# A table of powers moved into an accumulation bank, and the state product put into the bank of the query-key products

## The chip, the core and the metric

The kernel runs on one core of one Trainium2 chip. The metric is the device time of one execution in microseconds (us), the median of several executions. A core has five engines here: PE (TensorE, matrix products), DVE (VectorE), ACT (ScalarE), POOL (GpSimd) and SP (SyncE, which issues the DMAs). Each works through its own list of instructions in order. PE writes into eight accumulation banks (PSUM), all else that the engines read and write lies in SBUF.

## The reference

Three layers, one after the other, in float32, for a batch of 4, 768 positions, 8 heads of 48:

```python
for t in range(S):                                  # attention with a decaying state, per head
    kt, vt, rt = k[:, :, t], v[:, :, t], r[:, :, t]
    cur = einsum('bhd,bhe->bhde', u * kt, vt)
    y[:, :, t] = einsum('bhd,bhde->bhe', rt, state + cur)
    state = w[:, :, None] * state + einsum('bhd,bhe->bhde', kt, vt)
x = y as (4, 768, 384)
h = maximum(x @ w_in, 0); u, v = halves of h        # gate over positions, width 1024 -> 512
v_n = (v - mean) / sqrt(var + 1e-6)
x = (u * (w_spatial @ v_n + b_spatial)) @ w_out
h = maximum(x @ w_in2, 0)                           # gate with a convolution of 3 positions
x = (h * sigmoid(conv(h, conv_w))) @ w_out2
```

## The kernel before, in words

The attention is cut into 24 chunks of 128 positions, 6 for each batch entry. Chunk n has its queries and keys transposed in `ld[n]` (112 partitions: two heads of 48 with 16 unused between them; 4 pairs of heads by 128 positions), and queries, keys and values by position in `nat[n]`. The decay inside a chunk is put into tables of powers of `w`: `TT[:, 0]` for the queries, w to the power t - 64, and `TT[:, 1]` for the keys, w to the power 63 - t, which is the first one read backwards. A chunk goes through these steps:

- `scaled` (L569): the queries by their table on VectorE (L574), the keys by theirs on GpSimd (L583). For chunk 0 both at once on VectorE (L578).
- `bonus` and `keys` (L586, L604): GpSimd forms r*k*u (L591, L593) and scales the keys for the state (L606); VectorE sums the former (L249), and ScalarE lays the sums on the diagonal of `aT` (L254).
- `products` (L211): 8 products of keys and queries into two banks, `pa[0]` for the first head of each pair and `pa[1]` for the second. `masked` (L618) then copies each bank's valid triangle into `aT` on VectorE (L621).
- `outer` (L235): the product of keys and values over the chunk into the bank `pu`; `state` (L677) adds it to `zc` on VectorE (L683, L685), and ScalarE copies `zc` into `zbd` (L245) once `from_state` has read the old one; GpSimd decays `zc` (L692).
- `from_state` (L219) and `from_chunk` (L225): the result, summed in the bank `py`, which ScalarE and VectorE then split into two parts (L658 to L662).

The eight banks are all given away: three to the big products, one to the conversion of the weights, four to the attention (`pa[0]`, `pa[1]`, `py`, `pu`).

All other products of the kernel are done three times on such split parts. s1 (L709) and s2 (L755) multiply the attention's result by `w_in`, s3 (L776) goes over the positions, s4 (L800) multiplies by `w_out`, s5 (L878) and s6 (L921) are the second gate. The weights of the first gate come as 64-bit floats and are converted bit by bit on VectorE (L427 to L430) before they are split by ScalarE and GpSimd (L362, L364).

The order on every engine is set when the program is built: `Order` is a planner that goes through the steps with costs (`vector(cols)` is cols/960 + 0.17 us, `pairs(us)` is given by hand), and gives each engine the waiting step of lowest rank. `need` waits for keys that other steps announce by `done`. `od.chain` sets steps of TensorE one behind the other up to their `FORK`: one chain of `att_a` (the products, L609) and one of `att_v` (state product, from_state, from_chunk; L624). Where the planner has nothing for TensorE in its first 62 us, `keep_warm` (L558) puts in products of the identity that nobody reads. Other work comes into the gaps by rank, so the attention of later batch entries runs among the big products.

Of the kernel before, what the change touches and what calls it, by code (L numbers as in the profile page):

```python
# [26 lines left out]
class Order:  # L27
# [13 lines left out]
    @staticmethod  # L41
    def need(*keys):
        return "need", keys
# [42 lines left out]
    def spawn(self, g, rank=1, at=None):  # L86
        self._go(g, rank, self.t if at is None else at, None)
# [61 lines left out]
class Net:  # L149
# [28 lines left out]

    def att_psum(self, ps):
        C, NP = self.C, self.NP  # L180
        self.pa = [ps.tile([C, NP, C], F32, name=f"pa{i}") for i in range(2)]
        self.py = ps.tile([self.R, NP, C], F32, name="py")
        self.pu = ps.tile([self.R, NP, self.D], F32, name="pu")
        self.nc.vector.memset(self.py, 0.0)
        self.nc.vector.memset(self.pu, 0.0)

# [161 lines left out]
    def run(self, xd=None):  # L348
# [130 lines left out]
        if xd is None:  # L479
            ac = right("ac", 1)  # L480
            ld_p, nat_p = right("ld", 3), right("nat", 3)
            ew_p, at_p, ys_p = right("ew", 2), right("at", 2), right("ys", 2)
            TT = ac.tile([R, 2, NP, C], F32, name="TT")
            W128 = ac.tile([R, NP, 1], F32, name="W128")
            mask = ac.tile([C, C], U32, name="mask")
            maskb = mask.rearrange("c (o t) -> c o t", o=1).to_broadcast([C, NP, C])
            yd = dram.tile([n_chunks, R, 2 * C], F32, name="yd")
            W128b = W128.to_broadcast([R, NP, D])
# [19 lines left out]
        def tables():  # L508
# [14 lines left out]
            nc.vector.memset(wk, 1.0)  # L523
            self.att_psum(att.enter_context(tc.tile_pool(name="ps_a", bufs=1, space=PSUM)))

# [12 lines left out]
            nc.vector.reciprocal(out=iv, in_=asc[:, :, HALF:HALF + 1])  # L538
            nc.vector.tensor_tensor(TT[:, 0, :, 0:HALF], asc[:, :, 0:HALF], ivb, ALU.mult)
            nc.vector.tensor_tensor(TT[:, 1, :, HALF:C], dsc[:, :, 1:HALF + 1], ivb, ALU.mult)  # L540
            nc.scalar.activation(out=TT[:, 0, :, HALF:C], in_=asc[:, :, 0:HALF], func=ACTF.Copy)
            nc.scalar.activation(out=TT[:, 1, :, 0:HALF], in_=dsc[:, :, 1:HALF + 1], func=ACTF.Copy)

            for p in range(NP):
                nc.scalar.activation(
                    out=dw[:, p], in_=self.ident[0:R, 0:R], func=ACTF.Copy, scale=W128[:, p])
            self.transpose_table(TT[:, 1], dw)

# [20 lines left out]
        def scaled(n):  # L569
            yield need(("ldd", n))  # L570
            if n:
                spawn(scaled_k(n), rank(n))
                yield dve(NP * C)
                nc.vector.tensor_tensor(ld[n][:, 0], ld[n][:, 0], TT[:, 0], ALU.mult)  # L574
                done(("lq", n))
            else:
                yield dve(2 * NP * C)
                nc.vector.tensor_tensor(ld[n], ld[n], TT, ALU.mult)  # L578
                done(("lq", n), ("lk", n))

        def scaled_k(n):
            yield gps(NP * C)
            nc.gpsimd.tensor_tensor(ld[n][:, 1], ld[n][:, 1], TT[:, 1], ALU.mult)  # L583
            done(("lk", n))
# [24 lines left out]
        def att_a(n):  # L609
            yield need(("lq", n), ("lk", n))  # L610
            yield need(("A", n - 1, 0), ("A", n - 1, 1))
            yield od.pairs(1.0)
            self.products(ld[n][:, 0], ld[n][:, 1])
            for x in range(2):
                spawn(masked(n, x), rank(n))
            yield FORK

# [6 lines left out]
        def att_v(n):  # L624
            b, c = divmod(n, NCH)
            on = c < NCH - 1
            yield need(("lq", n), ("kn", n), ("z", n - 1))
            if on:
                yield od.pairs(0.45)
                self.outer(nat[n][:, 1], nat[n][:, 2])  # L630
                spawn(state(n), rank(n))
            yield need(("y", n - 1))
# [3 lines left out]
            done(("mix", n))  # L636
            yield need(("A", n, 0), ("A", n, 1))
            if c % HC == 0:
# [38 lines left out]
        def state(n):  # L677
            first = n % NCH == 0
            if not first:
                yield need(("zw", n - 1))  # L680
            yield dve(NP * D)
            if first:
                nc.vector.tensor_copy(out=self.zc, in_=self.pu)  # L683
            else:
                nc.vector.tensor_tensor(self.zc, self.zc, self.pu, ALU.add)  # L685
            yield need(("mix", n))
            yield act(2 * NP * D, 2)
            self.set_state()
            done(("z", n))
            if n % NCH < NCH - 2:  # L690
                yield gps(NP * D)
                nc.gpsimd.tensor_tensor(self.zc, self.zc, W128b, ALU.mult)  # L692
                done(("zw", n))
# [265 lines left out]

        done(("A", -1, 0), ("A", -1, 1), ("z", -1), ("y", -1))  # L960
        by_gat = gat_p, "g", gat_f, 2 * HT
# [39 lines left out]
        if xd is None:  # L1001
# [4 lines left out]
            for n in range(3):  # L1006
                spawn(load(n), rank(n))
                spawn(scaled(n), rank(n))
                spawn(bonus(n), rank(n))
            for g in (att_a, att_v):  # L1010
                spawn(od.chain([(g(n), rank(n)) for n in range(n_chunks)]), 0)
        else:
# [110 lines left out]
```

## Time and profile before

| what | value |
|---|---|
| median of 3 executions | 602.54 us (599.0 to 602.73) |
| profiled execution, its own time | 605.17 us |
| its span, first to last instruction | 603.1 us |
| PE busy | 577.6 us (96%) |
| DVE, ACT, POOL busy | 382.3, 356.5, 291.2 us |
| granted TensorE clock, mean over the span | 0.976 |

The profile is of one execution. The span is what lies between its first and its last instruction; the rest of its own time lies around it. Busy time counts an engine's instructions, not the waits between them.

### The profile page before, as it was taken

To read this page: it belongs to the slowest core of one execution; us is meant where nothing else is said; L and a number is where in the kernel's file an instruction comes from. 1 tells how busy PE (TensorE), PEld (TensorE's weight loads), DVE (VectorE), ACT (ScalarE), POOL (GpSimd) and SP (SyncE) were. 2 spreads that over 40 slices of the span, in tenths; PEclk is the share of its full clock that TensorE was granted. 3 is DMA by queue.
4 is the path that set the end of the run, shared out by engine and by line. 5 is a ranking of instruction groups with operands and counts; after the bars stand their busy time and mean duration, and the time that the engine had idled before them with its cause. 6 is when DMAs were issued, how large, how long until landed. Compare 5 with 4: busy or idle time off the path is not lost.

```text
span 603.1 us, 11155 instructions
## 1 busy us (share of the span) xinstructions
PE 577.6 (96%) x3980; PEld 546.3 (91%) x3980; DVE 382.3 (63%) x864; ACT 356.5 (59%) x877; POOL 291.2 (48%) x315
## 2 busy tenths in 40 slices
PE   6999969999999999999999999999999999999992
PEld 3999858999888999888999999999999999999991
DVE  4889878867679847778665533675546455564701
ACT  3558766736586456486354524487667666675810
POOL 5688877855858329468414240254223243232410
PEclk8999969999999999999999999999999999999997
DMA  8676545546565456285346714340221303120010
GB/s 219 209 218 210 153 158 163 172 140 212 156 194 195 114 165 217 57 265 160 120 166 238 261 59 139 150 158 27 93 84 49 106 13 106 57 76 27 15 39 33
DMA packets 49316, 81.29 MB, mean 135 GB/s; under 512 B 5601, under 2 KB 40930, under 8 KB 48866
## 3 DMA queue, kind: packets, MB, share of 16 engines
q1 hardware_dynamic: 49250, 80.48, 42.3%
q8 instruction: 33, 0.54, 0.4%
q14 instruction: 33, 0.27, 0.1%
HBM read 57.27 MB, written 23.20 MB: 133 GB/s over the span
## 4 chain that ended last, share of the span: by engine, by line
PE 88%; POOL 3%; DMA 3%; DVE 2%; issue 1%; ACT 1%; SPq 0%; ACTq 0%; DVEq 0%; POOLq 0%
PE s L887 17%; PE s L933 17%; PE s L784 15%; PE s L720 9%; PE s L810 8%; PE s L764 7%; PE pa L216 4%; PE warm L565 4%; PE py L231 4%; PE py L222 2%; DMA ld<-in_rkT_dram 1%; PE pu L239 1%; DMA nat<-in_rkv_dram 1%; POOL nat L591 1%; POOL ld L583 1%
## 5 line engine op out<-in xcount | busy, mean ns | idle before, releaser
L364 POOL TENSOR_TENSOR g<-g,g 128x384 fp32r<-128x384 f32 x64 | 64.6, 1014 | 122.6 <-ACT g L362 122.6
L887 PE MATMUL s<-xl,wi 128*128 128x386 f32 x576 | 108.1, 340 | 0.0
L933 PE MATMUL s<-wo,g 128*128 128x384 f32 x576 | 107.0, 339 | 0.0
L784 PE MATMUL s<-wsp,vn 128*128 128x384 f32 x576 | 104.3, 337 | 0.4 <-POOL vn L364 0.4
L887 PEld LDWEIGHTS s<-xl,wi 128*128 128x128 f32 x576 | 102.5, 189 | 0.0
L933 PEld LDWEIGHTS s<-wo,g 128*128 128x128 f32 x576 | 102.1, 188 | 0.0
L784 PEld LDWEIGHTS s<-wsp,vn 128*128 128x128 f32 x576 | 99.7, 188 | 2.4 <-POOL vn L364 0.8
L900 DVE SCALAR_TENSOR_TENSOR c<-h,cw,c 128x384 f32<-128x384 f32 x64 | 39.7, 621 | 57.6 <-ACT c L898 57.6
L254 ACT ACTIVATE aT<-ident,dg 128x128 f32<-128x128 f32 x192 | 60.1, 392 | 9.3 <-DVE dg L249 9.0
L364 POOL TENSOR_TENSOR gat<-u,gat 128x384 fp32r<-128x384 f32 x32 | 32.6, 1027 | 53.7 <-ACT gat L362 49.4
L720 PE MATMUL s<-wi,xT 128*128 128x512 f32 x216 | 57.2, 415 | 0.0
L764 PE MATMUL s<-xT,wi 128*128 128x384 f32 x288 | 54.7, 338 | 0.0
L810 PE MATMUL s<-gat,wo 128*128 128x384 f32 x288 | 53.3, 337 | 0.0
L764 PEld LDWEIGHTS s<-xT,wi 128*128 128x128 f32 x288 | 50.0, 188 | 1.0 <-ACT zbd L245 0.2
L810 PEld LDWEIGHTS s<-gat,wo 128*128 128x128 f32 x288 | 50.0, 188 | 0.6 <-ACT zbd L245 0.2
L720 PEld LDWEIGHTS s<-wi,xT 128*128 128x128 f32 x216 | 41.6, 198 | 9.5 <-issue 0.2
L903 ACT ACTIVATE c<-c 128x384 f32<-128x384 f32 x64 | 29.7, 465 | 31.5 <-DVE c L901 31.5
L907 DVE TENSOR_TENSOR g<-h,c 128x384 f32<-128x384 f32 x64 | 35.2, 551 | 19.9 <-ACT c L903 18.8
L895 ACT ACTIVATE h<-s 128x386 f32<-128x386 f32 x64 | 31.3, 489 | 17.1 <-PE s L887 15.9
L901 DVE SCALAR_TENSOR_TENSOR c<-h,cw,c 128x384 f32<-128x384 f32 x64 | 39.9, 623 | 2.3
L591 POOL TENSOR_TENSOR nat<-nat 128x384 f32<-128x384 f32 x24 | 24.9, 1039 | 31.6 <-DMA nat<-in_rkv_dram 23.3
L364 POOL TENSOR_TENSOR stg<-stg 128x192 fp32r<-128x192 f32 (+1 forms) x34 | 19.8, 587 | 41.2 <-ACT stg L362 35.7
(103 smaller groups left out, 932.1 us busy)
## 6 DMA issues: line engine op xcount, KB each, us to landing
nat<-in_rkv_dram SPq DMA_DIRECT2D x24, 576.0 KB, 4.2
ld<-in_rkT_dram SPq DMA_DIRECT2D x24, 448.0 KB, 5.4
xl<-x2d SPq DMA_DIRECT2D x8, 1155.0 KB, 6.1
x2d<-x SPq DMA_DIRECT2D x24, 384.0 KB, 3.0
stg<-in_w_out_dram SPq DMA_DIRECT2D x24, 192.0 KB, 2.8
out_dram<-o SPq DMA_DIRECT2D x24, 192.0 KB, 1.9
stg<-in_w_in_dram SPq DMA_DIRECT2D x12, 256.0 KB, 3.9
wo2d<-stg SPq DMA_DIRECT2D x16, 192.0 KB, 1.9
```

The costliest lines, as they stand in the source:

```text
L254: self.nc.scalar.activation(out=a[:, x, h // 2], in_=self.ident, func=ACTF.Copy, scale=d[:, h:h + 1])
L364: nc.gpsimd.tensor_tensor(dst[1], src, dst[0].bitcast(F32), ALU.subtract)
L720: nc.tensor.matmul(out=ps, lhsT=xt[:, k, l], rhs=wi[:, k, r, UF:DFF], start=(k == 0 and (l, r) == PARTS[0]), stop=(k == KD - 1 and (l, r) ...
L764: nc.tensor.matmul(out=ps, lhsT=wi[:, k, l, f * 128:(f + 1) * 128], rhs=xT[b, h][:, k, :, r], start=(k == 0 and (l, r) == PARTS[0]), stop= ...
L784: nc.tensor.matmul(out=ps, lhsT=vn[:, s, l, f * 128:(f + 1) * 128], rhs=wsp[:, s, r, h * HT:(h + 1) * HT], start=(s == 0 and (l, r) == PAR ...
L810: nc.tensor.matmul(out=ps, lhsT=wo[:, k, l, m * 128:(m + 1) * 128], rhs=gat[b, h, k][:, r], start=(k == 0 and (l, r) == PARTS[0]), stop=(k ...
L887: nc.tensor.matmul(out=ps, lhsT=late["wi2"][:, k, l, f * 128:(f + 1) * 128], rhs=xl[j][:, k, r], start=(k == 0 and (l, r) == PARTS[0]), st ...
L895: nc.scalar.activation(out=h, in_=ps, func=ACTF.Relu)
L900: nc.vector.scalar_tensor_tensor(c, h[:, 0:HT], cw[:, f, 0:1], c, ALU.mult, ALU.add)
L901: nc.vector.scalar_tensor_tensor(c, h[:, 2:HT + 2], cw[:, f, 2:3], c, ALU.mult, ALU.add)
L907: nc.vector.tensor_tensor(g, h[:, 1:HT + 1], c, ALU.mult)
L933: nc.tensor.matmul(out=ps, lhsT=g2[j][:, k, l, t * 128:(t + 1) * 128], rhs=late["wo2"][:, k, r], start=(k == 0 and (l, r) == PARTS[0]), st ...
```

## The change

The queries' table becomes a tile of its own, `TQ`, in an accumulation bank, and the keys' table a tile `TK` in SBUF. The bank for `TQ` is that of `pu`; `pu` becomes the first 192 columns of `pa[0]`. For this the state product leaves `att_v` and becomes a step `att_o` in the chain of the products, behind `att_a` of the same chunk; it waits until the first mask has read `pa[0]`, and the next chunk's products wait until `state` has read it (`zc`). from_chunk waits for it as well (`o`). Chunk 0's queries and keys are scaled by two instructions in place of one, the keys by the queries' table read backwards. The memset of `pu` is gone. The branch for other decays (`any_decay`, not run with these inputs) keeps its own `pu`.

```diff
-    def att_psum(self, ps):
+    def att_psum(self, ps, own=True):
...
-        self.pu = ps.tile([self.R, NP, self.D], F32, name="pu")
         self.nc.vector.memset(self.py, 0.0)
-        self.nc.vector.memset(self.pu, 0.0)
+        if own:
+            self.pu = ps.tile([self.R, NP, self.D], F32, name="pu")
+            self.nc.vector.memset(self.pu, 0.0)
+        else:
+            pu = self.pa[0].rearrange("c p t -> c (p t)")[0:self.R, 0:NP * self.D]
+            self.pu = pu.rearrange("r (p d) -> r p d", p=NP)
...
-            TT = ac.tile([R, 2, NP, C], F32, name="TT")
+            TK = ac.tile([R, NP, C], F32, name="TK")
+            TT = {}
...
+            TQ = TT["q"] = ps_a.tile([R, NP, C], F32, name="TQ")
...
         def scaled(n):
             yield need(("ldd", n))
-            if n:
+            late_k = n
+            if late_k:
                 spawn(scaled_k(n), rank(n))
+            yield dve(NP * C)
+            nc.vector.tensor_tensor(ld[n][:, 0], ld[n][:, 0], TT["q"], ALU.mult)
+            done(("lq", n))
+            if not late_k:
                 yield dve(NP * C)
-                nc.vector.tensor_tensor(ld[n][:, 0], ld[n][:, 0], TT[:, 0], ALU.mult)
-                done(("lq", n))
-            else:
-                yield dve(2 * NP * C)
-                nc.vector.tensor_tensor(ld[n], ld[n], TT, ALU.mult)
-                done(("lq", n), ("lk", n))
+                nc.vector.tensor_tensor(ld[n][:, 1], ld[n][:, 1], TT["q"][:, :, ::-1], ALU.mult)
+                done(("lk", n))
...
         def att_a(n):
             yield need(("lq", n), ("lk", n))
-            yield need(("A", n - 1, 0), ("A", n - 1, 1))
+            yield need(("A", n - 1, 0), ("A", n - 1, 1), ("zc", n - 1))
...
+        def att_o(n):
+            if n % NCH == NCH - 1:
+                done(("zc", n), ("o", n))
+                return
+            yield need(("kn", n), ("A", n, 0))
+            yield od.pairs(0.45)
+            self.outer(nat[n][:, 1], nat[n][:, 2])
+            done(("o", n))
+            spawn(state(n), rank(n))
+            yield FORK
...
             yield need(("lq", n), ("kn", n), ("z", n - 1))
-            if on:
-                yield od.pairs(0.45)
-                self.outer(nat[n][:, 1], nat[n][:, 2])
-                spawn(state(n), rank(n))
...
-            yield need(("A", n, 0), ("A", n, 1))
+            yield need(("A", n, 0), ("A", n, 1), ("o", n))
...
                 nc.vector.tensor_tensor(self.zc, self.zc, self.pu, ALU.add)
+            done(("zc", n))
...
-            for g in (att_a, att_v):
-                spawn(od.chain([(g(n), rank(n)) for n in range(n_chunks)]), 0)
+            for gs in ((att_a, att_o), (att_v,)):
+                spawn(od.chain([(g(n), rank(n)) for n in range(n_chunks) for g in gs]), 0)
```

## Rows read from the trace of the kernel before

In the timeline the columns are: start in us from the span's start, us, engine, line, operation, tiles written and read, shapes, count, and in brackets how long the engine was idle before and what ended that. PEld is the load of the stationary operand.

**Rows 1.** Busy time by stretch: us, busy by engine (instructions), PEclk, DMA share, GB/s.
```profile
60.00:100.00 40.00, 33.52 (x289) 28.78 (x291) 33.22 (x84) 26.29 (x73) 31.67 (x35) 0.83 0.52 150
100.00:150.00 50.00, 50.00 (x404) 46.67 (x399) 37.73 (x85) 32.59 (x96) 33.51 (x36) 1.00 0.59 183
```

**Rows 2.** Groups by line, the filler: busy us, mean ns, idle before.
```profile
L565 PE MATMUL warm<-ident 128*128 128x128 f32 x196 | 25.4, 287 | 0.0
```

**Rows 3.** TensorE's waits: line, releaser, us in total, times, longest us.
```profile
PE py L231 <- DVE rs L740: 5.0, 1, 5.0
...
PE pa L216 <- POOL vn L364: 1.5, 1, 1.5
PE pa L216 <- POOL gat L364: 1.2, 1, 1.2
```

**Rows 4.** Timeline around the three pauses of TensorE.
```profile
72.66 1.65 DVE L574 TENSOR_TENSOR ld<-ld,TT 112x512 f32<-112x512 f32 x1
...
74.41 1.16 PE L216 MATMUL pa<-ld 48*128 48x128 f32 x16 [1.45 <-POOL vn L364]
...
81.24 1.28 ACT L254 ACTIVATE aT<-ident,dg 128x128 f32<-128x128 f32 x4
...
81.65 2.94 DVE L574 TENSOR_TENSOR ld<-ld,TT 112x512 f32<-112x512 f32 x1
81.81 1.26 POOL L583 TENSOR_TENSOR ld<-ld,TT 112x512 f32<-112x512 f32 x1
...
83.04 1.00 POOL L593 TENSOR_TENSOR nat<-nat,uB 128x384 f32<-128x384 f32 x1
...
84.51 0.72 DVE L621 COPY_PREDICATED aT<-mask,pa 128x512 f32<-128x512 uint32 x1
...
85.28 1.94 PE L231 MATMUL py<-aT,nat 128*48 128x128 f32 x14 [5.03 <-DVE rs L740]
...
241.97 3.06 DVE L574 TENSOR_TENSOR ld<-ld,TT 112x512 f32<-112x512 f32 x1
...
245.13 1.16 PE L216 MATMUL pa<-ld 48*128 48x128 f32 x16 [1.21 <-POOL gat L364]
```

**Rows 5.** Single lines of VectorE: shortest/median/longest ns, first and last start; then by group.
```profile
L574 DVE TENSOR_TENSOR ld<-ld,TT x23: 684/1158/3064, 14.5 to 280.1; 112x512 f32<-112x512 f32 x23
...
L907 DVE TENSOR_TENSOR g<-h,c x64: 542/553/556, 375.7 to 572.0; 128x384 f32<-128x384 f32 x64
...
L791 DVE TENSOR_TENSOR s<-s,bB x32: 550/566/567, 108.8 to 384.4; 128x384 f32<-128x384 f32 x32
...
L574 DVE TENSOR_TENSOR ld<-ld,TT 112x512 f32<-112x512 f32 x23 | 32.9, 1431 | 2.5 <-DMA ld<-in_rkT_dram 2.5
...
L578 DVE TENSOR_TENSOR ld<-ld,TT 112x1024 f32<-112x1024 f32 x1 | 1.5, 1523 | 4.7 <-DMA ld<-in_rkT_dram 4.7
```

**Rows 6.** Busy time by stretch, columns as in group 1, two stretches behind pauses.
```profile
76.20:79.40 3.20, 3.20 (x8) 2.52 (x9) 2.77 (x6) 1.28 (x4) 3.20 (x4) 0.50 1.02 324
...
83.00:93.00 10.00, 7.72 (x53) 6.45 (x54) 7.81 (x20) 5.06 (x15) 5.42 (x7) 0.50 0.46 134
```

**Rows 7.** Timeline of chunk 4's state product, masks and addition, and chunk 5's products.
```profile
59.90 0.56 PE L239 MATMUL pu<-nat 128*48 128x48 f32 x16
...
62.45 1.38 DVE L621 COPY_PREDICATED aT<-mask,pa 128x512 f32<-128x512 uint32 x2
...
63.70 0.35 DVE L685 TENSOR_TENSOR zc<-zc,pu 112x192 f32<-112x192 f32 x1
...
66.14 1.16 PE L216 MATMUL pa<-ld 48*128 48x128 f32 x16
```

**Rows 8.** Timeline of chunk 21's masks, chunk 22's products and what follows on TensorE.
```profile
275.98 1.34 DVE L621 COPY_PREDICATED aT<-mask,pa 128x512 f32<-128x512 uint32 x2
...
276.81 1.72 PE L216 MATMUL pa<-ld 48*128 48x128 f32 x16
...
278.45 1.88 PE L720 MATMUL s<-wi,xT 128*128 128x512 f32 x7
```

More of the change, by code (lines that the diff above doesn't have):

```diff
@@ L523, in tables @@
             nc.vector.memset(wk, 1.0)
-            self.att_psum(att.enter_context(tc.tile_pool(name="ps_a", bufs=1, space=PSUM)))
+            ps_a = att.enter_context(tc.tile_pool(name="ps_a", bufs=1, space=PSUM))
+            self.att_psum(ps_a, False)
+            TQ = TT["q"] = ps_a.tile([R, NP, C], F32, name="TQ")
             for _ in range(4):
@@ L538, in tables @@
             nc.vector.reciprocal(out=iv, in_=asc[:, :, HALF:HALF + 1])
[L539 to L542, printed above, removed]
+            nc.vector.tensor_tensor(TQ[:, :, 0:HALF], asc[:, :, 0:HALF], ivb, ALU.mult)
+            nc.vector.tensor_tensor(TK[:, :, HALF:C], dsc[:, :, 1:HALF + 1], ivb, ALU.mult)
+            nc.scalar.activation(out=TQ[:, :, HALF:C], in_=asc[:, :, 0:HALF], func=ACTF.Copy)
+            nc.scalar.activation(out=TK[:, :, 0:HALF], in_=dsc[:, :, 1:HALF + 1], func=ACTF.Copy)
             for p in range(NP):
@@ L546, in tables @@
                     out=dw[:, p], in_=self.ident[0:R, 0:R], func=ACTF.Copy, scale=W128[:, p])
-            self.transpose_table(TT[:, 1], dw)
+            self.transpose_table(TK, dw)
         def masks():
@@ L570, in scaled @@
             yield need(("ldd", n))
-            if n:
+            late_k = n
+            if late_k:
                 spawn(scaled_k(n), rank(n))
+            yield dve(NP * C)
+            nc.vector.tensor_tensor(ld[n][:, 0], ld[n][:, 0], TT["q"], ALU.mult)
+            done(("lq", n))
+            if not late_k:
                 yield dve(NP * C)
-                nc.vector.tensor_tensor(ld[n][:, 0], ld[n][:, 0], TT[:, 0], ALU.mult)
-                done(("lq", n))
-            else:
-                yield dve(2 * NP * C)
-                nc.vector.tensor_tensor(ld[n], ld[n], TT, ALU.mult)
-                done(("lq", n), ("lk", n))
+                nc.vector.tensor_tensor(ld[n][:, 1], ld[n][:, 1], TT["q"][:, :, ::-1], ALU.mult)
+                done(("lk", n))
         def scaled_k(n):
             yield gps(NP * C)
-            nc.gpsimd.tensor_tensor(ld[n][:, 1], ld[n][:, 1], TT[:, 1], ALU.mult)
+            nc.gpsimd.tensor_tensor(ld[n][:, 1], ld[n][:, 1], TK, ALU.mult)
             done(("lk", n))
@@ L958, in in_turn @@
                 spawn(g, rank(i))
-        done(("A", -1, 0), ("A", -1, 1), ("z", -1), ("y", -1))
+        done(("A", -1, 0), ("A", -1, 1), ("z", -1), ("y", -1), ("zc", -1))
         by_gat = gat_p, "g", gat_f, 2 * HT
```

## The prediction, made before the result was known

> **What bounds the kernel now.** I read the stages first, then what TensorE waited for, then the minutes around each pause, and last the engine that ended the pause. From 100 us on TensorE has no gap worth naming: 50.00 of 50 us are busy in the second stretch of [rows 1], and the work in them is fixed by the shapes. Only the first 100 us can be shortened much. Before that TensorE often looks full, but much of it is filler: 196 warming products, busy for 25.4 us in all [rows 2], whose count the planner fixes when the program is built. Between 60 and 100 us VectorE (33.2 of 40) and GpSimd (31.7 of 40) are nearly full, TensorE is idle for 6.5 us and its granted clock is 0.83 [rows 1].
>
> TensorE's list of waits after the tables names three pauses: 5.0, 1.5 and 1.2 us [rows 3]. The names beside them (a small step of the norm, two GpSimd splits) are inferred, and mislead. In the timeline all three have the same cause: the multiplication of the queries by their table, L574 on VectorE. It is the wait one step back.
> - Chunk 6: L574 starts at 72.66 and takes 1.65 us; the products that need it start at 74.41, where L574 has just ended [rows 4].
> - Chunk 6 again: L574 for chunk 8 starts at 81.65 and takes 2.94 us; the mask L621 stands behind it in VectorE's queue and starts at 84.51; TensorE, in the middle of from_chunk, goes on at 85.28 [rows 4].
> - Chunk 20: L574 starts at 241.97, takes 3.06 us and ends at 245.03; the products start at 245.13 [rows 4].
>
> The same L574 of 112x512 takes 684 ns at its shortest, 1158 in the middle and 3064 at its longest, while L907, also a multiplication of two tensors but with one operand in an accumulation bank, stays between 542 and 556 ns in 64 instructions, and L791, with one operand in a bank and GpSimd at work beside it, between 550 and 567 in 32 [rows 5]. So L574 is the one VectorE instruction of the steady work with both inputs in SBUF, and it waits for GpSimd: the long one at 81.65 outlasts L583 and L593 on GpSimd, which end at 83.07 and 84.04 [rows 4].
>
> The Trainium skill (SBUF — State Buffer, Summary: rules for kernel authors) says that a VectorE instruction with two SBUF inputs and a GpSimd instruction that reads SBUF exclude each other, and that the later one waits until the first has finished. The trace agrees on the exclusion and not on the length: 2.25 us over the shortest at 81.65 is more than the rest of any one GpSimd instruction. By the page's length the second pause would hardly shorten.
>
> **The change part by part.**
>
> *The queries' table in a bank.* The 23 multiplications L574 then have one SBUF input. Price of one: L907 takes 553 ns for 384 columns [rows 5]; L574 has 128 columns more, and its shortest is 684, 131 ns above that, 1.02 ns for each of them: no sign that an operand in a bank costs more. I take 684. In total 32.9 us (23 at 1.43, [rows 5]) become 15.7. Most of the 17.2 us lie beside a full TensorE list and give nothing; what counts is the three pauses:
> - chunk 6, products: 1.65 - 0.68 = 0.97 us earlier, of a pause of 1.45.
> - chunk 6, mask: L574 would end at 82.33. What is late next is ScalarE's diagonal, L254 at 81.24, done at 82.52 [rows 4]; so the mask ends at 82.52 + 0.72 = 83.24 in place of 85.23: 1.99 us.
> - chunk 20: L574 would end at 242.65, before TensorE is free at 243.92: the whole 1.2 us.
>
> Sum 4.2 us.
>
> The Trainium skill (VectorE: DVE Perf Modes, The TRN2 errata) speaks against this part: reading an accumulation bank carries a fixed part of 120 cycles against 58 for SBUF. By it, an estimate from that page, each L574 would be 65 ns longer and the sum 0.2 us smaller; the rows of L907 against L574's shortest show no such difference.
>
> *The clock after the pauses.* From 76.2 to 79.4 and from 83 to 93 us the granted clock is 0.50, the lower of the two levels (1.2 GHz); before the first fall TensorE had the 1.45 us pause, before the second the 5.0 us one [rows 6]. The price at that level, by the windows: 3.20 us busy in the first, which at the upper level is 1.6 less, and 7.72 in the second, 3.9 less [rows 6]. Together 5.5 us if both falls vanish, 0 if both stay. The first pause would shrink to 0.5 us, the second to about 3; I take half, 2.7.
>
> *The state product in pa0.* Its 16 instructions (0.56 us, [rows 7]) are not changed, only placed: after the first mask, not after the previous state. The old outer product waited for no mask. Now outer(n) waits on TensorE for masked(n,0), and products(n+1) wait until VectorE has added the bank to the state; behind either, all of TensorE's in-order list is queued, the large products of the gate included, and behind products(n+1) both masks and so from_chunk. From the end of mask 0 the new path is 0.56 + 0.35 and three handovers of about 0.1 us each (L574 ends at 74.31, the products start at 74.41, [rows 4]): 1.2 us. In the trace, the products of the next chunk come 3.0 us or more after the end of the first mask in the first five chunks; chunk 4 is the closest: masks from 62.45 (two in 1.38), products at 66.14 [rows 7]. Over all 20 chunks with a state product only chunk 21 has less than 1.2: the masks start at 275.98, the next products at 276.81 [rows 8]. There the products move by about 1.1 us, covered by the products of the gate (L720) that follow at 278.45 [rows 8], and cost 1.1 without that cover. Lower bound 0 (the new state is not copied for the products before from_state of the same chunk has read the old one, and that comes later anyway); upper bound one more pause as the worst seen with its slow stretch, 5.0 + 3.9 = 8.9. I take 0.5, near the lower end, since all rows but one have the slack.
>
> *The first chunk.* One multiplication of 1024 columns, 1.52 us beside GpSimd [rows 5], becomes two of 0.68. Reading a table backwards has no row; by L574's shortest and mean it is 0.68 to 1.43, so -0.15 to +0.6 us on the start of TensorE's list, which begins with these products. I take 0.
>
> *Tables and the dropped memset.* VectorE waits 4.7 us for the first load behind the tables [rows 5]; writing one of them to a bank hides there. 0.
>
> *The planner.* It lays out every queue anew, SP's and GpSimd's too. It always counted 0.70 us for L574 (512/960 + 0.17), so its layout was right but for the waits; after the change the chip does what it planned. The filler can grow or shrink with the new links; the slack above says little: 0, with 3 us either way in the range.
>
> Sum: 4.2 + 2.7 - 0.5 = 6.4 us. The profiled execution took 605.17 (span 603.1 and 2.07 around it) and would take 598.8. The median of the runs shown is 602.54, 2.6 less than the profiled one; with the same saving it is 596.1.
>
> **The rivals.**
> 1. *The new chain of waits takes over, slower.* The path from products over mask, state product and addition to the next products binds in the first 100 us, where VectorE's queue is full. For: the addition of chunk 4 starts 3.2 us after its state product has ended (63.70 against 60.46, [rows 7]), as it stands in line. Against: the slack above. It decides once the addition lies more than 3.0 us behind the mask. Price: a pause of 5.0 with 3.9 of slow clock at two of the five chunks of the start that hand a state on, 17.8, against 4.2 + 2.7 gained: 10.9 slower, 613.4.
> 2. *The pauses move.* L574 is quicker, but the new order puts another late instruction (the diagonal on ScalarE at 82.52) before the same spots, and the clock falls as before. For: the second pause keeps 3 us in my own working. Gain 0 to 3, time 599.5 to 602.5, say 601.
> 3. *It does not do what it says*: the multiplication waits for GpSimd all the same, because of its output. Against it stand the narrow spreads of L907 and L791 [rows 5]. 602.5, less or more by the new order.
>
> **How the numbers follow.** Forecast (gain 3 to 11): 0.56, its own range 591.5 to 599.5. Rival 2: 0.25. Rival 1: 0.16. Rival 3: 0.03. Runs of this kernel spread from 599.0 to 602.73, so 1% (6 us) is about what a measurement can tell from no change. Of the forecast, 0.45 lies under 596.5; the rest of it and rivals 2 and 3 give 0.39; slower by over 1% is rival 1, 0.16. The range, 591 to 606, takes in rivals 2 and 3 with the filler's 3 us, and leaves out rival 1 and 0.04 for gains in which both falls of the clock and the filler come together.
>
> **What would show it.** L574's line: 23 at about 684 ns, longest under 750; GpSimd's L583 with no instruction of 1.7 us. TensorE's waits: no pause at products whose queries were just scaled. The windows from 60 to 100 us: granted clock over 0.9 and idle time under 4 us. The state product starts after the first mask in every chunk, and its addition before the next products. Filler about 196. The prediction is wrong if L574 still spreads, or if TensorE's list of waits names the state's addition or the mask for several us, or if the filler grows by tens.

## The result

The changed kernel takes 604.29 us (median of 18 executions, 601.92 to 607.15), the kernel before in the same set 600.52 us (median of 18, 598.62 to 605.67): a ratio of 1.0052, 95% interval 1.003 to 1.0075. A second set of the unchanged copy on another chip gave 1.0016 (0.9991 to 1.004). So the change gains nothing, and costs between nothing and 0.75%. Forecast were 596.1 us and a gain of 1%; the time lies in the range, 8.2 us above the forecast. Ratios and means, here and below, leave out the few executions of a slower state.

One thing about the times first. The profiled execution of before took 605.17, among the longest of its 18. The profiled one of after took 604.42, a usual one. The two traces differ by less than the two kernels do, the other way round.

What the prediction said of the table came true. Single lines of the changed kernel, columns as in [rows 5]:

```profile
L584 DVE TENSOR_TENSOR ld<-ld,TQ x24: 676/680/690, 10.5 to 270.7; 112x512 f32<-112x512 f32 x24
...
L588 DVE TENSOR_TENSOR ld<-ld,TQ x1: 681/681/681, 11.1 to 11.1; 112x512 f32<-112x512 f32 x1
...
L593 POOL TENSOR_TENSOR ld<-ld,TK x23: 1267/1291/1306, 14.2 to 271.0; 112x512 f32<-112x512 f32 x23
```

The queries' multiplication (now L584) has lost its spread: 690 ns at the longest, where L574 had gone to 3064. GpSimd's own multiplication (L593) stays under 1.31 us. Reading the table backwards for chunk 0 (L588) costs the same 681 ns. VectorE is busy for 365.7 us instead of 382.3.

Busy time by stretch, columns as in [rows 1]; the third stretch is the end of s1 and the third product of the last batch entry, where part of the loss lies:

```profile
60.00:100.00 40.00, 35.80 (x302) 31.32 (x301) 34.48 (x97) 30.81 (x84) 33.80 (x38) 1.00 0.53 163
100.00:150.00 50.00, 50.00 (x460) 45.19 (x459) 32.69 (x74) 31.00 (x92) 33.25 (x36) 1.00 0.61 186
...
340.00:352.00 12.00, 10.54 (x48) 9.54 (x47) 4.40 (x17) 4.58 (x9) 3.56 (x3) 0.86 0.62 209
```

From 60 to 100 us TensorE is idle for 4.2 us, where the profiled execution of before had 6.5 (another execution of before, b_again below, has 4.3, so this is not the change's doing). Its granted clock there is 1.00 (the 2.4 GHz level) where it was 0.83. But from 340 to 352 us, long after the attention, 1.46 of 12 us are idle and the clock is 0.86. Before has 0.45 us idle there, at a clock of 1.00:

```profile
340.00:352.00 12.00, 11.55 (x63) 10.84 (x62) 5.32 (x19) 5.56 (x11) 2.81 (x3) 1.00 0.76 257
```

TensorE's waits in after, columns as in [rows 3]:

```profile
PE s L738 <- DMA xT<-yd: 3.3, 2, 1.7
...
PE s L802 <- POOL vn L369: 1.3, 2, 0.7
PE py L227 <- DVE xT L679: 0.9, 1, 0.9
PE py L236 <- DVE aT L642: 0.9, 1, 0.9
```

The three pauses of [rows 3] are gone, and no line names the state's addition. In their place stand two waits of the first gate (L738) for the attention's result on its way through DRAM, 1.6 and 1.7 us, and two of the spatial product (L802) for a GpSimd split.

### The profile page after: what moved, and what is told of

The parts are those of the page before. It is cut to its first block, busy times and chain, and to the rows that moved or that the text cites. A ratio compares the mean times of both kernels' runs of the same rounds, so it can differ in the third digit from the quotient of the medians.

```text
span 602.7 us, 11220 instructions
## 1 busy us (share of the span) xinstructions
PE 578.3 (96%) x4000; PEld 544.6 (90%) x4000; DVE 365.7 (61%) x864; ACT 357.3 (59%) x877; POOL 282.2 (47%) x315
## 4 chain that ended last, share of the span: by engine, by line
PE 91%; DMA 3%; DVE 2%; ACT 1%; issue 1%; POOL 0%; SPq 0%; DVEq 0%; ACTq 0%
PE s L905 17%; PE s L951 17%; PE s L802 17%; PE s L738 8%; PE s L828 8%; PE s L782 8%; PE warm L574 5%; PE pa L221 4%; PE py L236 4%; PE py L227 3%; DMA ld<-in_rkT_dram 2%; PE pa L244 2%; DMA xT<-yd 0%; ACT v L764 0%; DMA wt<-in_w_dram 0%
## 5 line engine op out<-in xcount | busy, mean ns | idle before, releaser
L802 PE MATMUL s<-wsp,vn 128*128 128x384 f32 x576 | 106.8, 341 | 1.5 <-POOL vn L369 1.3
L802 PEld LDWEIGHTS s<-wsp,vn 128*128 128x128 f32 x576 | 101.0, 190 | 4.2 <-POOL vn L369 2.0
L738 PE MATMUL s<-wi,xT 128*128 128x512 f32 x216 | 54.2, 399 | 3.3 <-DMA xT<-yd 3.3
L738 PEld LDWEIGHTS s<-wi,xT 128*128 128x128 f32 x216 | 39.4, 188 | 12.3 <-ACT v L764 2.0
L369 POOL TENSOR_TENSOR vn<-v,vn 128x512 fp32r<-128x512 f32 x24 | 30.8, 1288 | 28.9 <-ACT vn L367 28.4
L642 DVE COPY_PREDICATED aT<-mask,pa 128x512 f32<-128x512 uint32 x48 | 34.8, 741 | 14.5 <-PE pa L221 10.3
```

Source lines behind the costliest of these rows:

```text
L369: nc.gpsimd.tensor_tensor(dst[1], src, dst[0].bitcast(F32), ALU.subtract)
L642: nc.vector.copy_predicated(aT[n][:, x], maskb, self.pa[x])
L738: nc.tensor.matmul(out=ps, lhsT=xt[:, k, l], rhs=wi[:, k, r, UF:DFF], start=(k == 0 and (l, r) == PARTS[0]), stop=(k == KD - 1 and (l, r) ...
L802: nc.tensor.matmul(out=ps, lhsT=vn[:, s, l, f * 128:(f + 1) * 128], rhs=wsp[:, s, r, h * HT:(h + 1) * HT], start=(s == 0 and (l, r) == PAR ...
```

## The experiments

Four sets, each with the kernel before on the same chip. Ratios are to that kernel, with their 95% intervals; the kernel before had medians of 602.77, 602.0, 602.0 and 601.24 us.

| run | what | median us | ratio (interval) | mean clock | at 0.982, us |
|---|---|---|---|---|---|
| after | the first set, as above | 604.29 | 1.0052 (1.003 to 1.0075) | 0.985 | 605.5 |
| b_again | before, unchanged | 601.62 | 0.9967 (0.9937 to 0.9996) | 0.983 | 602.4 |
| a_sbuf | after, TQ in SBUF | 606.83 | 1.007 (1.0034 to 1.0105) | 0.985 | 608.7 |
| a_u50 | after, less filler | 605.59 | 1.0048 (1.0015 to 1.0081) | 0.984 | 606.5 |
| a_hold | after, one product held back | 601.97 | 0.9971 (0.9943 to 1.0) | 0.987 | 604.3 |
| b_early | before with after's order at the end of s1 | 603.23 | 1.0008 (0.9974 to 1.0042) | 0.983 | 603.5 |
| b_onein | before, L574 with one input | 607.52 | 1.0084 (1.0053 to 1.0114) | 0.977 | 605.1 |
| a_hold2 | after, two products held back | 600.5 | 0.9962 (0.9931 to 0.9993) | 0.989 | 603.5 |
| a_hold_sbuf | a_hold, TQ in SBUF | 606.34 | 1.0084 (1.0053 to 1.0114) | 0.986 | 608.7 |
| a_again | after, unchanged | 602.77 | 1.0016 (0.9991 to 1.004) | 0.988 | 605.4 |
| a_hold_own | a_hold_sbuf, state product in its own bank | 606.24 | 1.0071 (1.0046 to 1.0097) | 0.987 | 608.0 |
| b_hold | before, one product held back | 601.75 | 1.0 (0.9964 to 1.0036) | 0.982 | 601.6 |
| a_dma26 | a_hold2, planner counts 2.6 us for a DMA | 601.64 | 0.9991 (0.9968 to 1.0013) | 0.986 | 603.1 |
| b_memset | before, L574 a memset | 599.06 | 0.9946 (0.9928 to 0.9965) | 0.982 | 598.7 |
| b_mhold | b_memset and b_hold | 599.23 | 0.996 (0.994 to 0.9979) | 0.981 | 598.8 |
| a_mhold | a_hold2 with the memset | 600.29 | 0.9987 (0.9969 to 1.0005) | 0.988 | 603.1 |

The line of b_again is the measure for the others: an unchanged kernel came out 0.33% off. A single difference of 0.4% proves little; what follows rests on several runs that agree, or on what a trace shows.

Much of that scatter is the granted clock, of which every execution has a mean over its span. Among the executions of one kernel in one set, a mean clock higher by 0.01 goes with a time that is 4.4 us shorter (a straight line through 315 executions in 20 groups). The last column, "at one clock" in what follows, is an estimate from it: the mean time of a version, moved to a clock of 0.982, the mean of the kernel before. There the kernel before comes out at 602.6, 602.1, 602.0 and 602.0 in the four sets (602.2 over all, clock 0.981 to 0.984) and at 602.4 as b_again; after, 0.36% apart by its two ratios, comes out at 605.5 and 605.4. The values are uncertain by 0.3 to 1.1 us.

### Where is the loss: the table, the filler or the end of s1?

The filler grew from 196 to 216 warming products, by groups of lines in after:

```profile
L574 PE MATMUL warm<-ident 128*128 128x128 f32 x216 | 28.5, 289 | 0.0
```

**b_again**, an unchanged copy of before:

> The kernel before once more, for a second profile of it: the first one (605.17 us) was among its slowest executions, the median of 18 is 600.5. If the two falls of the granted clock between 76 and 93 us belong to every execution, the span is again near 603 and the falls are there; if they belong to slow executions only, the span is 598 to 600, the clock stays at 1.00 from 60 to 100 us, and the 5.5 us that the prediction hoped to get back from the clock were never there to get. L574 spreads from 0.68 to 3 us in either case. The ratio to the kernel before is 1.000.

L574 and its pauses are there as in [rows 3, 5], but the clock of the first stretch differs from [rows 1]; busy time by stretch, b_again:

```profile
60.00:100.00 40.00, 35.70 (x300) 31.04 (x299) 35.15 (x92) 30.43 (x86) 35.41 (x38) 0.91 0.58 174
```

It is 0.91 in place of 0.83: one fall of the clock in that stretch of this execution, two in the one that was read for the prediction. TensorE's idle time there is 4.3 us (40 - 35.70) where that one had 6.5.

**a_u50** ends the filler earlier, which takes the 20 added products away and leaves the rest of the order alone:

```diff
-            spawn(keep_warm(62.0), 9)
+            spawn(keep_warm(50.0), 9)
```

> The changed kernel without the five filler pairs that its planner lays between the products of chunk 5 and from_state of chunk 5 (67.51 to 70.01 us); 98 pairs are left, as in the kernel before, and all else keeps its order. If the filler holds up the work behind it: 2.4 us faster than the changed kernel, 602. If from_state of chunk 5 has to wait for the last split of chunk 4 anyway (it ended at 69.64): same as the changed kernel, 604.3, or slower if the clock falls in the pause.

No gain (1.0048 against 1.0052). TensorE's timeline in a_u50 shows why; columns as in [rows 4]:

```profile
65.43 1.16 PE L221 MATMUL pa<-ld 48*128 48x128 f32 x16
68.80 1.10 PE L227 MATMUL py<-ld,zbd 112*112 112x128 f32 x8 [2.20 <-DVE rs L758]
```

Without the 2.5 us of filler, TensorE stands still for 2.20 us at the same place, before from_state of chunk 5. The filler only covered a wait. But the wait is one of the new order, as the timelines of the same place in before and in after show:

```profile
67.23 3.40 PE L764 MATMUL s<-xT,wi 128*128 128x384 f32 x18
...
67.51 2.50 PE L574 MATMUL warm<-ident 128*128 128x128 f32 x20
```

Between the products and from_state of chunk 5 the old order has 18 products of s2 to do, the new one nothing but filler.

**a_sbuf** puts the table back into SBUF, in after's order:

```diff
-            TQ = TT["q"] = ps_a.tile([R, NP, C], F32, name="TQ")
+            TQ = TT["q"] = ac.tile([R, NP, C], F32, name="TQ")
```

> The changed kernel with the queries' table in SBUF again, every queue in the same order. If the table in the bank is worth something and the new order is what costs: 2 to 5 us slower than the changed kernel, 606 to 609 (ratio to the kernel before 1.010 to 1.015), L584 spreading up to 3 us again and TensorE pausing behind it. If the table's waits lay beside other work all along: 604.3, as the changed kernel, ratio 1.005 to 1.007.

The spread came back with the table in SBUF, single lines of a_sbuf:

```profile
L584 DVE TENSOR_TENSOR ld<-ld,TQ x24: 683/968/3845, 10.6 to 272.9; 112x512 f32<-112x512 f32 x24
```

So the bank alone is what ends the waits. Yet the time is only 0.2% above a_u50 and after's first set, 0.5% above its second (a_again). At one clock it is 3.2 us above after and 2.2 above a_u50. Busy time by stretch, a_sbuf:

```profile
60.00:100.00 40.00, 35.76 (x308) 30.77 (x307) 36.69 (x97) 30.38 (x83) 35.52 (x37) 1.00 0.53 160
```

Its granted clock there is 1.00 as in after, with the waits back in place, so the restored clock of that stretch came mostly with the new order, not with the bank. (a_hold_own, below, has 0.96 there, also without the bank.)

**a_hold** goes to the end of s1 in the last batch entry. The timeline of TensorE there in before:

```profile
338.18 4.24 PE L720 MATMUL s<-wi,xT 128*128 128x512 f32 x18
342.26 1.75 PE L764 MATMUL s<-xT,wi 128*128 128x384 f32 x9
343.84 2.24 PE L810 MATMUL s<-gat,wo 128*128 128x384 f32 x12
345.92 3.11 PE L784 MATMUL s<-wsp,vn 128*128 128x384 f32 x17
349.48 3.76 PE L784 MATMUL s<-wsp,vn 128*128 128x384 f32 x20 [0.45 <-POOL vn L364]
```

And in after:

```profile
336.08 4.28 PE L738 MATMUL s<-wi,xT 128*128 128x512 f32 x18
340.20 2.27 PE L828 MATMUL s<-gat,wo 128*128 128x384 f32 x12
342.31 3.01 PE L802 MATMUL s<-wsp,vn 128*128 128x384 f32 x14
...
346.06 0.79 PE L802 MATMUL s<-wsp,vn 128*128 128x384 f32 x3 [0.74 <-POOL vn L369]
347.42 6.86 PE L802 MATMUL s<-wsp,vn 128*128 128x384 f32 x29 [0.58 <-POOL vn L369]
```

The last 18 products of s1 give the last two chunks of `vn`; their norm and split take until GpSimd has done, and s3 of that batch entry needs them. In before 7.1 us of other products lie in between (1.75 + 2.24 + 3.11), 9 products of s2 among them. In after the planner has put these 9 ahead of s1, so only 5.3 us are left (2.27 + 3.01). TensorE pauses for 0.74 and 0.58 us in place of 0.45. Behind the pauses the clock fell: 0.86 over the 12 us shown above. The edit holds these 9 products back until s1 has been issued (the first line at the end of s1, the others at the start of s2):

```diff
+            done(("s1", b, c))
...
+            if (b, h, f) == (3, 1, 1):
+                yield need(("s1", b, NCH - 1))
```

> The changed kernel with one of the 32 s2 products (the sixth of the last batch entry) held back until the last s1 product, so that it stands before the last batch's s3 as in the kernel before; all else keeps its order. If TensorE runs dry there (pauses of 0.73 and 0.58 us at 345 and a clock of 0.50 for 3.4 us from 348): the pauses and the fall are gone, 2 to 3 us faster than the changed kernel, 601.5 to 602. If the loss lies in the new chain of waits earlier on: 604.3.

1.0052 became 0.9971; at one clock the gain is 1.2 us (604.3 against 605.5). The timeline in a_hold:

```profile
333.18 4.28 PE L738 MATMUL s<-wi,xT 128*128 128x512 f32 x18
337.30 2.27 PE L831 MATMUL s<-gat,wo 128*128 128x384 f32 x12
339.40 1.72 PE L785 MATMUL s<-xT,wi 128*128 128x384 f32 x9
340.96 3.20 PE L805 MATMUL s<-wsp,vn 128*128 128x384 f32 x17
344.89 1.33 PE L805 MATMUL s<-wsp,vn 128*128 128x384 f32 x6 [0.73 <-POOL vn L369]
```

The 9 products (L785) are back between s1 and s3, and one pause is left.

### Do both halves hold on their own?

**a_hold2** holds back two such sets, `(b, h) == (3, 1) and f < 2`:

> a_hold with two s2 products held back until the last s1 product in place of one. If a dry TensorE before the last s3 is what is left there (a pause of 0.72 us at 344 in a_hold): the pause is gone, 0.7 us faster than a_hold, ratio to the kernel before 0.995 to 0.997. If not: as a_hold, 0.997 to 0.998.

The pause at L805 is gone: from 342.87 on TensorE runs 53 products of s3 without a gap. 0.9962 is the best ratio of all versions that leave nothing out. Its lead over before, 0.38%, is hardly larger than the 0.33% by which an unchanged copy differed, and it comes with the clock: 0.989 in its executions, 0.982 in before's. At one clock it is 1.3 us slower than before.

**b_early** gives before the order that after has there, by holding the last s1 products until the 9 products of s2 are issued (in s1; s2 announces them):

```diff
+            if (b, c) == (3, 4):
+                yield need(("s2", 3, 1, 1))
```

> The kernel before with the opposite of a_hold: the same s2 product is done before the last two s1 products and not behind them, as the changed kernel does it; the table stays in SBUF, the state product in its own bank, all else in order. If the early s2 product is the cause of the loss: TensorE pauses twice before the last batch's s3 and the clock falls behind, 2.5 to 3 us slower than the kernel before, ratio 1.004 to 1.005, as large as the whole loss of the change. If a_hold won for another reason: ratio 1.000.

Here the trace and the time say different things. The trace repeats after's two pauses (0.73 and 0.58) and the clock of 0.86 from 340 to 352 us, where before has 1.00; the time, 1.0008, shows no loss that could be told from no change. At one clock, though, it is 1.5 us slower than before in its set (603.5 against 602.1), about what the two holds win in after (1.2 and 2.0 us). So the order makes the pauses, and they cost 1 to 2 us, not the 2.5 to 3 that were expected.

**b_onein** was meant to take GpSimd out of L574's way in before's own order, by a multiplication with a number, so the queries' decay is left out:

> The kernel before, its order unchanged, with L574 made an instruction with one input in SBUF (it multiplies the queries by 1 in place of the table: the decay of the queries is left out for all chunks but the first). It stands for the table in a bank without the new order. If the waits of L574 cost what the prediction counted: no L574 over 0.75 us, the pauses of 1.3, 2.3 and 2.5 us shortened by 3 to 4 us together, ratio 0.993 to 0.996. If they are mostly made up for elsewhere, as a_sbuf against the changed kernel (1 to 2.5 us) says: ratio 0.996 to 0.999.

It failed as an instrument, single lines of b_onein:

```profile
L575 DVE TENSOR_SCALAR ld<-ld x23: 718/1252/4985, 14.1 to 279.1; 112x512 f32<-112x512 f32 x23
```

With one input it waits just as long, and the kernel is slower than before by 0.8%. Part of that goes with its clock, the lowest of all (0.977); at one clock 3 us are left, and why I did not isolate.

**a_hold_sbuf** is a_hold with the table in SBUF:

> a_hold with the queries' table in SBUF: the new order without the early s2 product and without the table in the bank. If the table in the bank is worth 1 to 2.5 us and the rest of the new order nothing: ratio 0.999 to 1.001, 1 to 2.5 us slower than a_hold. If the table is worth nothing once the loss at the end is taken out: as a_hold, 0.997.

1.0084, 1.2% above a_hold2 and 1.1% above a_hold: some 7 us for the bank, where the same edit without the hold (a_sbuf) seemed worth 0.2%. At one clock the two agree: 4.4 us here (608.7 against 604.3), 3.2 there (608.7 against 605.5), each uncertain by about 1 us. The rest of the difference is the granted clock, of these versions and of the kernel before beside them.

### Is it the new chain of waits, or the order?

**a_hold_own** gives the state product its own bank back, so that no instruction waits for the mask or the addition through the bank; the order stays that of a_hold_sbuf:

```diff
-            self.att_psum(ps_a, False)
+            self.att_psum(ps_a)
```

> a_hold_sbuf with the state product in a bank of its own again: the new order of every queue stays (without the early s2 product), the table stays in SBUF, but neither the state product waits for the mask nor the next products for the addition. a_hold_sbuf was 0.8% slower than the kernel before. If these new waits are what costs: 3 to 5 us less than a_hold_sbuf, ratio 1.000 to 1.003, and no pause at the state product. If it is the new order, which asks other work earlier than it can be had: as a_hold_sbuf, 1.007 to 1.010.

1.0071 against 1.0084: the chain of waits is not what costs. (The table must be in SBUF here, since no bank is left for it.) And since the table and the state product lie here where they lie in before (only chunk 0 is still scaled in two steps), this is the price of the new order by itself, although with the hold: 0.71%, 4.3 us, with an interval clear of no change (1.0046 to 1.0097). At one clock it is 5.8 us.

**a_again**, an unchanged copy of after:

> The changed kernel once more, on the chip of the other three. If the loss at the end of the last batch's s1 belongs to the order and not to one execution: the two pauses of 0.7 and 0.6 us before the last s3 are there again, with or without the fall of the clock behind them; ratio to the kernel before 1.003 to 1.0075 as before.

It has the same two pauses and the same idle time in the stretch from 340 to 352 us, but not the fall of the clock (busy time by stretch, a_again):

```profile
340.00:352.00 12.00, 10.53 (x57) 9.50 (x56) 5.30 (x20) 4.58 (x9) 3.56 (x3) 1.00 0.64 215
```

The pauses belong to the order; the fall behind them came in one execution and not in another.

**b_hold** puts the hold into before, where the set to hold is `(3, 1, 0)`:

> The kernel before with one more s2 product held back until the last s1 product (the fifth of the last batch entry; the sixth stands there already). It is the fair counterpart of a_hold2: what the old order wins by the same edit. The pause of 0.45 us before the last s3 goes and nothing else: 0.4 us, ratio 0.998 to 1.000. If the kernel before, too, wins 2 us by it, the edit and not the table is what made a_hold2 fast.

Nothing gained that could be told from no change (1.0): before has only a pause of 0.45 us to mend there.

**a_dma26** is a_hold2 with a planner that counts 2.6 us for a DMA in place of 2.0, so that the waits of L738 for the result through DRAM would be planned for:

> a_hold2 with the planner told that a DMA lands 2.6 us after its transfer in place of 2.0, which lays out the queues anew: in the changed kernel TensorE waits twice (1.6 and 1.7 us at 82 and 90) for the result that goes through DRAM. If these waits are the planner's optimism: they go, 2 to 3 us faster than a_hold2, ratio 0.990 to 0.994. If TensorE has no other work ready there: the pauses move, 0.996 or slower.

The waits moved and the gain did not come. TensorE's waits in a_dma26:

```profile
PE py L236 <- DVE rs L759: 2.4, 1, 2.4
PE s L738 <- DMA xT<-yd: 1.1, 1, 1.1
PE s L738 <- ACT stg L428: 1.0, 1, 1.0
```

Less for the DMA (1.1 us instead of 2.5 in a_hold2), but 2.4 at the mask again.

### What are the waits worth in the old order?

**b_memset** replaces L574 in before by a memset of the same tile, which nothing holds up; the queries of all chunks but the first are lost. The order is before's, to the instruction:

```diff
-                nc.vector.tensor_tensor(ld[n][:, 0], ld[n][:, 0], TT[:, 0], ALU.mult)
+                nc.vector.memset(ld[n][:, 0], 0.01)
```

> The kernel before, its order unchanged, with L574 replaced by a memset of the same 512 columns (the queries of all chunks but the first are lost; L184, the same shape, took 0.48 us, so 0.2 us less than a table in a bank). It reads nothing and stands for a table that never waits for GpSimd, in the old order. If the old order would have won what the prediction counted: the pauses of 1.3, 2.3 and 2.5 us behind L574 and the clock's falls go, 4 to 6 us faster than the kernel before, ratio 0.990 to 0.993. If the next late step stands right behind (the result of chunks 5 and 6 on its way through DRAM, for which the changed kernel waits twice): 0 to 2 us, ratio 0.996 to 1.000, with a pause of s1 for that DMA between 80 and 95 us.

0.9946: 0.54% of 601.24 us, 3.2 us (2.1 to 4.3 by the interval). With the hold, which gave before nothing, it came out at 0.996, 2.4 us (b_mhold, below); at one clock both are some 3.4 us below before. A single line of b_memset:

```profile
L574 DVE MEMSET ld<- x23: 485/485/485, 14.1 to 274.1; 112x512 f32 x23
```

Its longest pause of TensorE after the tables, in the list of waits:

```profile
PE py L231 <- DVE rs L740: 2.4, 1, 2.4
```

The timeline ahead of that pause:

```profile
78.43 1.28 ACT L254 ACTIVATE aT<-ident,dg 128x128 f32<-128x128 f32 x4
...
79.45 0.48 DVE L574 MEMSET ld<- 112x512 f32 x1 [0.53 <-DMA ld<-in_rkT_dram]
...
79.85 0.67 DVE L621 COPY_PREDICATED aT<-mask,pa 128x512 f32<-128x512 uint32 x1
...
80.58 1.94 PE L231 MATMUL py<-aT,nat 128*48 128x128 f32 x14 [2.38 <-DVE rs L740]
```

Of the three pauses of [rows 3] the two at the products are gone or small. The one at the mask has shrunk from 5.0 to 2.4 us plus one of 0.68 just ahead of it, and what it waits for now is ScalarE's diagonal: L254 ends at 79.71, the mask starts at 79.85. The clock fell there all the same; busy time by stretch, b_memset:

```profile
60.00:100.00 40.00, 35.86 (x312) 31.25 (x307) 33.08 (x94) 31.63 (x90) 33.28 (x38) 0.91 0.62 188
76.00:90.00 14.00, 10.94 (x75) 8.92 (x74) 10.80 (x31) 10.12 (x31) 10.47 (x13) 0.76 0.60 190
```

0.91 from 60 to 100 us is what b_again has with the waits in place, and over the whole span the executions of b_memset have a clock of 0.982 on average, before's in the same set 0.984: without the waits, the clock of the old order is no higher.

**b_mhold** adds the hold of b_hold, **a_mhold** is a_hold2 with the same memset (queries lost again):

> b_memset with one more s2 product held back until the last s1 product, as in b_hold: what the old order could reach without L574's waits and without a pause before the last s3. 0.4 us less than b_memset if the last pause is 0.45 as in the kernel before; nothing else should differ.

> a_hold2 with the same memset in place of the table's product: the measure for the two others. If the memset stands fairly for the table in a bank: as a_hold2, ratio 0.994 to 0.997. If it is faster by more, the 0.2 us less per chunk count and the two others have to be read with that.

a_mhold (0.9987) is no faster than a_hold2 with the real multiplication (0.9962), so the memset is a fair stand-in for a multiplication that doesn't wait. Between b_mhold and a_mhold, both without the wait and both with the hold, lie 0.27% (1.6 us) in favour of the old order; their intervals overlap. This is the net of two effects: at one clock the new order is 4.3 us slower (603.1 against 598.8), and its executions have the higher clock, 0.988 against 0.981.

## Why the prediction was wrong, point by point

- **The bound and the cause of the pauses** were right. L574 waited for GpSimd, the bank ends it, and a table back in SBUF brings it back (a_sbuf). 680 ns against the 684 taken. The 65 ns that the prediction held against this part did not show; by its own working they would have moved only the first pause, by 0.07 us and not 0.2.
- **The three pauses, 4.2 us**: 3.2 and 2.4 us measured by b_memset and b_mhold, 3.4 at one clock; in the new order the bank is worth 3.2 and 4.4 at one clock (a_sbuf, a_hold_sbuf). So this term was nearly right in either order. The second pause behaved as worked out: ScalarE's diagonal was next late, and about 3 us of pause stayed (0.68 + 2.38).
- **The clock, 2.7 us**: not won by ending the pauses. In the old order the fall behind the mask's pause stays, and the mean clock with it (b_memset). In the new order it is gone from 60 to 100 us, with the bank or without it (a_sbuf), and the mean clock is 0.985 and 0.988 (after, a_again) where before has 0.982: by 4.4 us for 0.01 a gain of 1.4 and 2.4 us. That its size is near the forecast is luck, since it comes from the order and not from the table. The profiled execution of before had two falls behind the pauses [rows 6] and was among the longest of 18; b_again had one in that stretch. A term read from one execution's clock was counted as if every execution had it.
- **The state product, -0.5 us**: small, as said. In each of the 20 chunks with a state product it starts after the first mask, and its addition ends before the next products start, at the closest by 0.2 us. For chunk 21, where 1.1 us were feared [rows 8], TensorE's and VectorE's timelines in after show:

```profile
266.26 0.56 PE L244 MATMUL pa<-nat 128*48 128x48 f32 x16
266.75 1.85 PE L782 MATMUL s<-xT,wi 128*128 128x384 f32 x9
269.13 1.16 PE L221 MATMUL pa<-ld 48*128 48x128 f32 x16 [0.53 <-issue]
...
268.08 0.35 DVE L702 TENSOR_TENSOR zc<-zc,pa 112x192 f32<-112x192 f32 x1
268.35 0.68 DVE L584 TENSOR_TENSOR ld<-ld,TQ 112x512 f32<-112x512 f32 x1
```

  The addition ends at 268.43, 0.7 us before the next products. The pause of 0.53 us ahead of them ends with L584, the queries of chunk 22, which stands behind the addition in VectorE's queue and ends at 269.03. a_hold_own puts no price on the chain that could be told from nothing.
- **The first chunk and the tables, 0**: right; 680 and 681 ns.
- **The planner, "0, with 3 us either way": this is the step that failed.** "After the change the chip does what it planned" was taken for granted, and only the filler was weighed. It also looked for nothing new behind 100 us, where its rows had shown no gap worth naming. The new order costs 4.3 us by itself (a_hold_own, 1.0071, with the table in SBUF and the hold), and from the sets after lies 0.7 to 1.1% above b_memset, 4 to 6 us. At one clock that is 6.8 us (605.5 against 598.7), against which stand the 3.4 us of the bank and the 1.4 to 2.4 of the clock. About 5 of the 6.8 can be seen in the traces. TensorE's waits behind the first products and the filler over the wait at chunk 5 add up to 9.4 us in after: 3.3 for the result through DRAM, 2.5 of filler, 1.3 ahead of the last s3, 2.3 in smaller ones. b_memset has 4.6. The pauses ahead of the last s3, where s2 stands before s1, lie 250 us behind the changed lines; the hold that undoes them gives back 1.2 to 2.0 us. The waits for the DMA moved when planned for (a_dma26), without a gain. With the hold and without L574's waits the new order is still 4.3 us behind the old at one clock (a_mhold, b_mhold), 1.6 as measured.
- **The rivals.** The first (a new chain of waits, slower) had the sign right and the mechanism wrong. The second (the pauses move) came nearest; only they moved to other work, not to the next late instruction at the same spots. The third was false.
- **The signs named beforehand.** Right: L584's line, GpSimd's line, the three pauses, the state product and its addition, the clock over 0.9. Missed: idle time 4.2 us against "under 4", and one pause at products whose queries were just scaled, the 0.53 us at chunk 22. And the filler grew by 20, which had been named as a sign of being wrong: it is not a cost by itself (a_u50), but it stands over a wait of 2.2 us that the new order brought.

Open is where the rest of the new order's price lies, some 2 of 6.8 us, and why the clock falls less often in the new order. That the new order costs when the table is contended is seen three times, at 1.007 to 1.0084 on three chips.

## What to carry to other kernels

When a list planner lays out the queues, an edit that frees one engine changes the order on all of them: before counting the gain, try the edit in the old order (a stand-in that doesn't wait is enough), and then look in the new order at what stands between the last producer of each phase and its first consumer. Count filler that grows as a wait. Read the price of a stall and of the clock behind it from several executions, since the one that was profiled may be an unusual one, and compare versions at one granted clock: one edit that looked worth 7 us in one place and 1 us in another turned out worth 4.4 and 3.2. A mend at the place that the trace names (two lines that hold back one set of products) gave back 1 to 2 us of what the order had cost.

## What the runs showed of the hardware that was not expected

- A VectorE multiplication with one SBUF input and a number, read and written in strides, waits for GpSimd like one with two inputs: 718/1252/4985 ns (b_onein) beside 684/1158/3064 [rows 5]. The Trainium skill (SBUF — State Buffer, Summary: rules for kernel authors) names two SBUF inputs or a two-port mode as the condition; whether this instruction ran in such a mode no run shows. A memset of the same tile does not wait: 485 ns, 23 times.
- The wait can be longer than such a GpSimd instruction: 4.27 us over the shortest in b_onein (4985 against 718 ns), where L593, one of the longer steps of GpSimd's steady work, takes 1.31 us at most in after. The same section of the Trainium skill lets the later instruction wait until the first has finished; here it was passed over: during the longest wait of b_onein, from 62.42 to 67.41 us, GpSimd ran four instructions one behind another (62.41 to 66.84).
- An operand in a bank cost this multiplication nothing more, and neither does reading it backwards: 680 and 681 ns beside 683 from SBUF (shortest of a_sbuf).
